# Linear attention into a two-layer tanh-shrink block: moving the phi and the loads of some token groups, and cutting w_out into 128-row loads

## The chip, the cores and the metric

The kernel runs on one core of a Trainium2 chip. The metric is the device time of one execution in microseconds (us). The text calls the engines by short names: PE is TensorE (matrix products), DVE is VectorE, ACT is ScalarE, POOL is GpSimd, SP is SyncE, which here only issues DMAs. POOL also issues DMAs: all loads of inputs. Each engine works off its own instructions in the order in which they were written; semaphores hold an instruction until what it reads is there.

## The reference

Eight batches, eight heads, 576 tokens, 64 features per head. A linear attention is followed by two matrix products over all 4608 tokens:

```python
def phi(x):
    return np.where(x > 0, x, np.exp(x) - 1.0) + 1.0
q_p, k_p = (phi(q), phi(k))
kv = np.einsum('bhsd,bhse->bhde', k_p, v)
z = np.sum(k_p, axis=2)
num = np.einsum('bhsd,bhde->bhse', q_p, kv)
den = np.einsum('bhsd,bhd->bhs', q_p, z)[..., None] + 1e-06
attn = num / den

x = attn.transpose(0, 2, 1, 3).reshape(4608, 512)
h = x @ w_in                  # w_in 512 x 2048
g = h - np.tanh(h)
out = g @ w_out               # w_out 2048 x 512
```

All inputs and the output are float32; the kernel computes in bfloat16 with float32 sums.

## The kernel before

**Chunks.** The 4608 tokens are worked in nine chunks of 512. Chunk c below 8 holds the first 512 tokens of batch c (each partition's first eight of nine tokens); chunk 8 holds the ninth token of every partition for all eight batches, 64 tokens a batch, which the code calls the rest. For batches 0 and 1 the main work leaves the ninth tokens of q out (`main(b)` is J - 1), and they are handled by `load_qr`, `r_phi`, `r_den`, `r_num` and `r_scale` later in the kernel.

**The loop over chunks** (lines 636 to 798). Layer 1 is 16 steps (`fi`, 0 to 15), one for each 128 features of the hidden layer: four matmuls of 128x128 by 128x512 (`l1mm`, line 463), then tanh on ACT and the subtraction on DVE, which give `gT`. From chunk 1 on two steps share one tanh and one subtraction (`l1act2`, lines 469 and 470); in chunk 0 each step has its own (`l1act`, lines 474 and 475). Layer 2 is 16 steps too, each of four matmuls (`l2mm`, line 484): they sum over the 16 blocks of 128 rows of `w_out` into one PSUM bank for each 128 tokens, and ACT copies the finished bank out (`evac`), from where SP stores it. So a layer is 64 large matmuls on PE.

**Work on other batches between the steps.** The lists `s1[i]` and `s2[i]` hold functions that are called behind step i of layer 1 or layer 2. In this way the attention of later batches is spread over the chunks: in chunk c the batch c + 2 gets its phi and its kv products, batch c + 1 its numerators. The position in the lists is the order in which the work stands in each engine's queue. phi is three instructions: exp on ACT (line 156), max and add on DVE (157), min on DVE (158). `a_num` (line 413) makes the numerators of a batch and, in the same place, the kv products of the next; its results lie in PSUM banks 0 to 3 and, for the rest tokens, 6 and 7, and ACT and DVE copy them to `xT`, the input of layer 1. For batches 3 and up the denominators are made by POOL and DVE: `q_prod` (two POOL multiplications, line 242), `q_den` (four DVE sums), `q_scale` (DVE reciprocal and two POOL multiplications, line 256, then the transposing DMA of line 175 that gives `qT`). For batches 0 and 1 PE spreads them (`b0_spread`, `a_spread_pe`), and for batch 2 they go through DRAM (`a_spread`, lines 405 and 408, tile `rdb`).

**Chunk 0** is different: its layer 2 takes its steps from `plan0(s)`, a list of (token block, first w_out block, end). In steps 0 to 3 it takes w_out blocks 0 to 3 for one token block each, in steps 4 to 7 blocks 4 to 7, in 8 and 9 blocks 8 and 9, in 10 and 11 one block for all four token blocks, and in 12 to 15 two blocks for two token blocks. Batch 1's whole attention is put in between these steps: phi of q behind steps 0 and 1, `prepare` (constants for the spreading) behind 2, phi of k behind 4 and 5, transposes of q on PE into banks 4 to 7 behind 5, kv products behind 9, denominators and numerators behind 10, spreading and scaling behind 13. Layer 1 of chunk 0 uses banks 0 to 7 in turn; its steps 12 to 15 use banks 4 to 7.

**Loads.** `load_rest` (line 528) issues on POOL, behind a gate that waits for a DVE instruction of batch 0: the last three quarters of w_in, w_out blocks 0 to 3, q of batch 1, w_out blocks 4 to 7, k of batch 1, blocks 8 and 9, v of batch 1 in two halves, and the last six blocks in four pieces. An issue on POOL waits until the eighth transfer before it has landed. Batches 2 and up are loaded by three issues (k, q, v) from lists: batch 2 behind step 5 of chunk 0's layer 2, batch 3 in chunk 1's layer 1, batch c + 3 behind step 9 of chunk c's layer 2, which for batch 4 is in chunk 1. The tiles `kraw` and `qraw` have one buffer each.

**The rest of batches 0 and 1.** `load_qr` (four issues) stands behind step 10 of chunk 4's layer 2; `r_phi` (one exp, two DVE instructions at lines 329 and 330, a transposing DMA at 332) behind step 9 of chunk 6's layer 1; `r_den` and `r_num` behind `a_num` at step 9 of chunk 6's layer 2. `r_den` writes columns 384 to 447 of bank 7, DVE reads them (line 343), and the result goes through DRAM (lines 348 and 352) to the tile `rdbr`. `r_num` writes columns 128 to 383 of banks 6 and 7. `r_scale`, behind step 3 of chunk 7's layer 1, puts both into `xT`.

Of the kernel before, what the change touches and what calls it, by code (L numbers as in the profile page):

```python
# [18 lines left out]
def kernel(  # L19
# [9 lines left out]
    nc = tc.nc  # L29
    B, H, S, D = q.shape  # L30
# [62 lines left out]
    def load(b, t, src, halves):  # L93

        n = main(b) if src is q else J
        x = src[b].rearrange("h (p j) d -> (h p) (j d)", j=J)[:, 0:n * D]
        if halves:
            y = x.rearrange("(h i q) x -> i q h x", h=2, i=2)
            for i in range(2):
                for hs in ((0, 1), (1, 2)) if i and src is k and b == 0 else ((0, 2),):  # L100
                    nc.gpsimd.dma_start(out=t[:, hs[0]:hs[1], i, 0:n].rearrange("q h j d -> q h (j d)"),
                                        in_=y[i, :, hs[0]:hs[1]])
        else:
            nc.gpsimd.dma_start(out=t[:, :, :, 0:n].rearrange("q h i j d -> q (h i) (j d)"),  # L104
                                in_=x.rearrange("(n q) x -> q n x", n=4))

    def load_k(b):
        k_t[b] = kpool.tile([128, 2, 2, J, D], BF16, name="kraw")
        load(b, k_t[b], k, b == 0)

    def load_q(b):
        q_t[b] = kpool.tile([128, 2, 2, J, D], BF16, name="qraw")
        load(b, q_t[b], q, b == 0)

    def load_v(b):
        load(b, v_b[b % 2], v, b < 2)

    def load_wi(f0, n):

        nc.gpsimd.dma_start(out=w_in_sb[:, :, f0:f0 + n],  # L120
                            in_=moe_w_in[:, f0:f0 + n].rearrange("(t p) f -> p t f", p=128))

    def load_wo(g):
        nc.gpsimd.dma_start(out=w_out_sb[:, 4 * g:4 * g + 4, :],
                            in_=moe_w_out[512 * g:512 * g + 512, :].rearrange("(ko ki) f -> ki ko f", ki=128))


    def load_wof(f0, n):
        nc.gpsimd.dma_start(out=w_out_sb[:, f0:f0 + n, :],
                            in_=moe_w_out[128 * f0:128 * (f0 + n), :].rearrange("(ko ki) f -> ki ko f", ki=128))  # L130
# [33 lines left out]
    def a_kphi(b, i):  # L164
        phi(b, k_t, kp_t, "kp", i)

    def a_qphi(b, i):
        phi(b, q_t, qp_t, "qp", i)
# [37 lines left out]
    def a_vp(b, i, eng=nc.vector):  # L206
        eng.tensor_copy(vp[:, i, :, :, 0:64].rearrange("p j h d -> p h j d"), v_b[b % 2][:, :, i])  # L207
# [320 lines left out]
    def load_rest(r):  # L528
        nc.gpsimd.tensor_copy(rpool.tile([1, 1], BF16, name="g0"), r[0:1, 1, J - 1, 63:64])
        for f0 in (512, 1024, 1536):  # L530
            load_wi(f0, 512)
        load_wo(0)
        load_q(1)
        load_wo(1)
        load_k(1)
        load_wof(8, 2)
        nc.gpsimd.memset(vp[:, :, :, :, 64:66], 1.0)
        load_v(1)
        for f0, n in ((10, 1), (11, 1), (12, 2), (14, 2)):
            load_wof(f0, n)  # L540

# [82 lines left out]

    def plan0(s):

        g, i = divmod(s, 4)
        if g < 2:
            return [(i, 4 * g, 4 * g + 4)]
        if s < 10:  # L630
            return [(n, 8, 10) for n in (2 * i, 2 * i + 1)]
        if s < 12:
            return [(n, s, s + 1) for n in range(4)]
        return [(n, 12 + 2 * (s % 2), 14 + 2 * (s % 2)) for n in (i - i % 2, i - i % 2 + 1)]

    for c in range(NC):
        gT = gpool.tile([128, NF, 512], BF16, name="gT")
# [3 lines left out]
        if c == 0:  # L641
            sub = {}

            def spread1():
                a_spread_pe(1, range(NP))
                for p in range(NP):
                    a_scale(1, p, sub["ns"], p)

            def kv1():
                kv_cols_mm(1, 4, 0)  # L650
                kz_copy(1, 4, 0)

            def num1():
                ns = sub["ns"] = new_ns(1)
                for i in (1, 0):
                    b0 = 4 + 2 * i
                    num_mm(1, i, lambda h: b0 + h)
                    nc.scalar.copy(ns[:, i::2, 0:8, :].rearrange("p a j t -> p a (j t)"), ps_all[:, b0:b0 + 2, :])

            s2[0].append(lambda: a_qphi(1, 0))  # L660
            s2[1].append(lambda: a_qphi(1, 1))
            s2[4].append(lambda: a_kphi(1, 0))
            def k1():
                ek, rk, mk = phi_pieces(1, k_t, kp_t, "kp", 1)
                ek()
                rk()
                a_vp(1, 0)
                mk()
                a_vp1(0, nc.vector.tensor_copy)
                a_vp1(1, nc.scalar.copy)  # L670

            s2[5].append(lambda: ([f() for i in range(2) for f in a_qT_pe(1, i, Banks([4 + 2 * i, 5 + 2 * i]))], k1(),
                                  load_q(2), load_k(2), load_v(2)))
            s2[2].append(prepare)
            s2[9].append(kv1)
            s2[10].append(lambda: (a_den(1, 4), num1(), a_split(1)))
            s2[13].append(spread1)

            qs, ks = [], []

            def exp2(pieces, src, store, name, i):
                pieces.append(phi_pieces(2, src, store, name, i))
                pieces[i][0]()

            def rest2(f):
                f[1]()
                f[2]()

            def k2(i):
                ks.append(phi_pieces(2, k_t, kp_t, "kp", i))  # L690
                ks[i][1]()

            s2[14].append(lambda: exp2(qs, q_t, qp_t, "qp", 0))
            s2[15].append(lambda: (exp2(qs, q_t, qp_t, "qp", 1), rest2(qs[0]), rest2(qs[1]), a_qT_dma(2), [f() for f in later], k2(0), k2(1)))
        elif n1 < B:
            if c == 1:
                def kv2():
                    kv_cols_mm(2, 6, 0)
                    kz_copy(2, 6, 0)

                s1[10].append(kv2)
            if n1 < QS:
                s1[12].append(lambda: (a_den(n1, 6), a_spread(n1)))
            else:
                if c == 2:
                    s1[2].append(lambda: (q_den(n1, 0, 0), q_den(n1, 0, 1)))
                e = 2 * (c == 2)
                s1[3 + e].append(lambda: q_den(n1, 1, 0))
                s1[5 + e].append(lambda: q_den(n1, 1, 1))
                s1[7 + e].append(lambda: q_scale(n1))  # L710
            m = 12 if c == 1 else 9
            s2[m].append(lambda: a_num(n1, n2 if n2 < B else 0))
            if c == B - 4:
                s2[m + 1].append(load_qr)
            if c == B - 2:
                s1[9].append(r_phi)
                s2[m].append(lambda: (r_den(7, 384), r_num(6, 128)))
            if n2 < B:
                s2[m + 2].append(lambda: (q_zb(n2, 4 if c == 1 else 7), q_prod(n2)))
                if c > 1:  # L720
                    s2[15].append(lambda: (q_den(n2, 0, 0), q_den(n2, 0, 1)))
# [8 lines left out]
        if c >= 1 and n2 < B:  # L730
            d = 2
            s2[d].append(lambda: a_kphi(n2, 0))
            s2[d + 2].append(lambda: a_kphi(n2, 1))
            s2[d + 4].append(lambda: a_qphi(n2, 0))
            s2[d + 6].append(lambda: a_qphi(n2, 1))
            for i in range(2):
                s2[d + 1 + 2 * i].append(lambda i=i: a_vp(n2, i))
            if n2 + 1 < B:
                s2[9].append(lambda: (load_k(n2 + 1), load_q(n2 + 1), load_v(n2 + 1)))
        if c == 0:  # L740

            first = Banks([4, 5, 6, 7, 0, 1, 2, 3])
# [34 lines left out]
        os_ = {}  # L777
        for s in range(16):

            (g, i) = divmod(s, 4) if c == 0 else (s % 4, s // 4)  # L780
            if g == 0:
                os_[i] = ps_all[:, i if c == 0 else 4 + i % 2, :]
            if c == NC - 1 and i == 3:

                if g == 0:
                    o2 = ps_all[:, 0, :]
                    for o, f in ((os_[i], slice(0, 384)), (o2, slice(384, DM))):
                        for fi in range(NF):
                            nc.tensor.matmul(o[:, f], gT[:, fi, 384:512], w_out_sb[:, fi, f],
                                             start=(fi == 0), stop=(fi == NF - 1))  # L790
                        evac(c, i, o, f.start, f.stop)
                continue
            for n, f0, f1 in plan0(s) if c == 0 else [(i, 4 * g, 4 * g + 4)]:
                l2mm(gT, os_[n], n, f0, f1)
                if f1 == NF:
                    evac(c, n, os_[n])
            for f in s2[s]:
                f()
# [30 lines left out]
```

## Time and profile before

| | us |
|---|---|
| timed runs, median (lowest to highest of 3) | 286.73 (286.54 to 286.74) |
| the profiled execution, its own time | 289.94 |
| span of that execution, first to last instruction | 288.2 |

The timed runs are other executions than the profiled one. The share of the span in which each engine was busy tells how near each is to its limit; the costliest groups of instructions are the two lines of large matmuls:

```profile
L484 PE MATMUL ps_all<-w_out_sb,gT 128*128 128x512 bf16 x541 | 124.1, 383 | 3.6 <-DVE gT L470 1.9
L463 PE MATMUL ps_all<-xT,w_in_sb 128*128 128x512 bf16 x550 | 122.3, 379 | 0.8 <-DVE xT L434 0.2
```

A row reads: line, engine, operation, output and inputs by the program's names, shape, count, then busy time in us and the mean length of one in ns, then the time for which the engine stood idle just before such instructions and what ended most of it. Matmuls overlap, so the mean of 383 ns is not the distance from one to the next. Some 3% of the matmuls have no record (541 and 550 of 560 each). Where a stretch of the span is shown, times count from the span's start.

Stages of the span by PE's work, in us (layer 1 is L1, layer 2 is L2):

| chunk | L1 from | L1 length | L2 length |
|---|---|---|---|
| 0 | 16.14 | 14.03 | 17.24 |
| 1 | 47.41 | 15.24 | 15.26 |
| 2 | 77.91 | 14.34 | 15.90 |
| 3 | 108.15 | 13.82 | 15.39 |
| 4 | 137.36 | 13.81 | 15.29 |
| 5 | 166.46 | 13.82 | 15.26 |
| 6 | 195.54 | 15.86 | 18.46 |
| 7 | 229.86 | 13.81 | 13.81 |
| 8 | 257.48 | 13.82 | 16.90 to the end |

### The profile page before, as it was taken

How to read it: one execution, taken by the hardware profiler on the slowest of the kernel's cores; microseconds unless marked ns; L12 is line 12 of the kernel's file. 1: busy time of each engine (PE TensorE's matmuls, PEld its weight loads, DVE VectorE, ACT ScalarE, POOL GpSimd, SP SyncE). 2: the span in 40 equal slices, each digit the busy share in tenths (PEclk: the TensorE clock that was granted, in tenths of full speed). 3: DMA queues.
4: the chain of work that ended last, by engine and by line, in shares of the span. 5: the costliest groups of instructions: out<-in, count | busy, mean ns of one | idle time of the engine just before them, and what ended most of it. 6: DMA issues, size and time to landing. Idle time of an engine off the chain costs nothing.

```text
span 288.2 us, 5067 instructions
## 1 busy us (share of the span) xinstructions
PE 275.8 (96%) x2055; PEld 131.6 (46%) x2085; DVE 179.2 (62%) x285; ACT 146.4 (51%) x177; POOL 81.3 (28%) x76
## 2 busy tenths in 40 slices
PE   8899999999999999999999999999977999999996
PEld 2564544444444454445444544454433444444443
DVE  5759877983878737874687468755963066106700
ACT  4747658856256735674556455654622156116511
POOL 8642220510544253514351744014410000000000
PEclk9999999999999999999999999999999799999999
DMA  7999999799990897069605990522053210131023
GB/s 106 182 206 207 206 206 196 162 193 190 257 226 11 99 210 170 0 122 212 143 0 118 174 203 1 121 56 55 0 100 75 73 38 2 36 73 36 2 61 85
DMA packets 40087, 33.25 MB, mean 115 GB/s; under 512 B 17696, under 2 KB 35776, under 8 KB 39936
## 3 DMA queue, kind: packets, MB, share of 16 engines
q0 software_dynamic: 18640, 18.35, 40.1%
q1 hardware_dynamic: 21424, 14.58, 21.8%
q8 instruction: 16, 0.26, 0.4%
q14 instruction: 7, 0.06, 0.1%
HBM read 38.14 MB, written 9.46 MB: 165 GB/s over the span
## 4 chain that ended last, share of the span: by engine, by line
PE 74%; DMA 12%; DVE 6%; issue 2%; ACT 2%; POOL 1%; SPq 1%; DVEq 0%; POOLq 0%
PE ps_all L463 37%; PE ps_all L484 32%; DMA v<-in_v_dram 3%; DMA rdb<-ds 3%; DVE gT L470 2%; DMA out_dram<-osb 2%; DMA qT<-qp 2%; DMA ds<-rden 2%; PE ps_all L203 1%; PE ps_all L750 1%; PE ps_all L284 1%; ACT th L469 1%; DVE xT L434 1%; DVE qpr L330 1%; ACT osb L495 1%
## 5 line engine op out<-in xcount | busy, mean ns | idle before, releaser
L484 PE MATMUL ps_all<-w_out_sb,gT 128*128 128x512 bf16 x541 | 124.1, 383 | 3.6 <-DVE gT L470 1.9
L463 PE MATMUL ps_all<-xT,w_in_sb 128*128 128x512 bf16 x550 | 122.3, 379 | 0.8 <-DVE xT L434 0.2
L470 DVE TENSOR_TENSOR gT<-ps_all,th 128x1024 bf16<-128x1024 f32 x64 | 77.6, 1217 | 46.1 <-ACT th L469 46.1
L469 ACT ACTIVATE th<-ps_all 128x1024 f32<-128x1024 f32 x64 | 65.6, 1025 | 48.7 <-PE ps_all L463 46.1
L463 PEld LDWEIGHTS <-w_in_sb 128*128 128x128 bf16 x560 | 54.6, 98 | 66.2 <-issue 1.0
L484 PEld LDWEIGHTS <-gT 128*128 128x128 bf16 x560 | 54.3, 99 | 66.4 <-issue 4.6
L495 ACT COPY osb<-ps_all 128x512 f32<-128x512 f32 (+1 forms) x36 | 20.8, 583 | 61.5 <-PE ps_all L484 49.4
L256 POOL TENSOR_TENSOR qp<-qp,rd 128x1152 bf16<-128x1152 bf16 x10 | 21.0, 2124 | 39.0 <-issue 23.1
L242 POOL TENSOR_TENSOR pr<-qp,zb 128x1152 f32<-128x1152 bf16 x10 | 23.5, 2372 | 18.8 <-ACT zb L235 18.8
L247 DVE TENSOR_REDUCE dn<-pr 128x9 f32<-128x576 f32 x20 | 14.5, 745 | 12.8 <-POOL pr L242 12.8
L156 ACT ACTIVATE e<-qraw 128x1152 bf16<-128x1152 bf16 (+1 forms) x16 | 18.1, 1135 | 3.2 <-DMA qraw<-in_q_dram 3.2
L156 ACT ACTIVATE e<-kraw 128x1152 bf16<-128x1152 bf16 x15 | 17.4, 1162 | 2.2 <-DMA kraw<-in_k_dram 2.2
L158 DVE TENSOR_TENSOR qp<-e,r 128x1152 bf16<-128x1152 bf16 (+1 forms) x16 | 11.9, 742 | 4.3 <-ACT e L156 3.2
L158 DVE TENSOR_TENSOR kp<-e,r 128x1152 bf16<-128x1152 bf16 x15 | 11.4, 760 | 4.7 <-ACT e L156 3.9
L104 POOL DMA_DIRECT2D kraw<-in_k_dram x7 | 5.4, 772 | 30.3 <-ACT e L156 14.1
L425 DVE CAST xT<-ps_all 128x1024 bf16<-128x1024 f32 x5 | 6.1, 1217 | 7.1 <-PE ps_all L293 7.1
L570 PE MATMUL ps_all<-zero 128*128 128x512 bf16 x28 | 8.5, 457 | 1.3 <-DVE zero L518 1.2
L104 POOL DMA_DIRECT2D qraw<-in_q_dram x7 | 5.5, 780 | 11.9 <-ACT e L156 7.1
L475 DVE TENSOR_TENSOR gT<-ps_all,th 128x512 bf16<-128x512 f32 x12 | 7.9, 688 | 0.9 <-ACT th L474 0.2
L207 DVE COPY vp<-v 128x1152 bf16<-128x1152 bf16 x11 | 5.7, 518 | 4.2 <-DMA v<-in_v_dram 4.2
L474 ACT ACTIVATE th<-ps_all 128x512 f32<-128x512 f32 x12 | 7.2, 598 | 2.3 <-DVE gT L756 1.0
L157 DVE TENSOR_SCALAR r<-qraw 128x1152 bf16<-128x1152 bf16 (+1 forms) x16 | 7.6, 476 | 0.3 <-DMA qraw<-in_q_dram 0.3
(109 smaller groups left out, 146.5 us busy)
## 6 DMA issues: line engine op xcount, KB each, us to landing
out_dram<-osb SPq DMA_DIRECT2D x65, 128.0 KB, 2.4
kraw<-in_k_dram POOLq DMA_DIRECT2D x7, 576.0 KB, 7.8
qraw<-in_q_dram POOLq DMA_DIRECT2D x6, 576.0 KB, 9.6
v<-in_v_dram POOLq DMA_DIRECT2D x6, 576.0 KB, 11.9
w_in_sb<-in_moe_w_in_dram POOLq DMA_DIRECT2D x3, 512.0 KB, 10.6
v<-in_v_dram POOLq DMA_DIRECT2D x4, 288.0 KB, 12.4
rdb<-ds SPq DMA_DIRECT2D x2, 576.0 KB, 5.8
w_out_sb<-in_moe_w_out_dram POOLq DMA_DIRECT2D x2, 512.0 KB, 16.0
```

The source lines that it names most:

```text
L104: nc.gpsimd.dma_start(out=t[:, :, :, 0:n].rearrange("q h i j d -> q (h i) (j d)"), in_=x.rearrange("(n q) x -> q n x", n=4))
L156: return (lambda: nc.scalar.activation(e, x, AF.Exp), lambda: nc.vector.tensor_scalar(r, x, 0.0, 1.0, ALU.max, ALU.add), lambda: nc.vector ...
L158: lambda: nc.vector.tensor_tensor(y, e, r, ALU.min))
L242: nc.gpsimd.tensor_mul(pr_t[b][:, i].rearrange("p j h d -> p j (h d)"), qp_t[b][:, i].rearrange("p j h d -> p j (h d)"), zb_t[b][:, i].uns ...
L247: nc.vector.tensor_reduce(dn_t[b][:, i, :, h], pr_t[b][:, i, :, h, :], mybir.AxisListType.X, ALU.add)
L256: nc.gpsimd.tensor_mul(x, x, rd[:, i].unsqueeze(2).to_broadcast([128, J * 2, D]))
L463: nc.tensor.matmul(h, w_in_sb[:, p, fi * 128:(fi + 1) * 128], xT[:, p, c * 512:(c + 1) * 512], start=(n == 0), stop=(n == NP - 1))
L469: nc.scalar.activation(th, h, AF.Tanh)
L470: nc.vector.tensor_sub(gT[:, fi:fi + 2, :], h, th)
L484: nc.tensor.matmul(o, gT[:, fi, i * 128:(i + 1) * 128], w_out_sb[:, fi, :], start=(fi == 0), stop=(fi == NF - 1))
L495: nc.scalar.copy(osb[:, f0:f1], o[:, f0:f1])
L570: nc.tensor.matmul(ps_all[:, 0, :], zero[:, 0:128], zero, start=True, stop=True)
```

## The change

Three places are changed.

1. The rest tokens of batches 0 and 1: `load_qr` goes from chunk 4's layer 2 to behind step 12 of chunk 3's layer 1; `r_phi` goes from chunk 6's layer 1 to behind step 1 of chunk 4's layer 2; `r_den` and `r_num` stay at step 9 of chunk 6's layer 2 but stand ahead of `a_num`.
2. Batch 4's three loads go from behind step 9 to behind step 15 of chunk 1's layer 2, so behind batch 3's `q_prod` in POOL's queue.
3. Chunk 0's layer 2 takes one 128-row block of w_out for all four token blocks in each of the steps 0 to 11; steps 12 to 15 stay. The loads follow: ten w_out transfers in place of seven, with q of batch 1 ahead of w_out. Batch 1's phi of q goes behind steps 13 and 14 of chunk 0's layer 1, its phi of k behind steps 0 and 3 of layer 2, its transposes behind step 2, `prepare` behind 4, the copies of v behind 6 and 8, and batch 2's three loads behind 2, 3 and 8.

```diff
@@ def load
-            for i in range(2):
+            for i in halves:
...
-        load(b, k_t[b], k, b == 0)
+        load(b, k_t[b], k, (0, 1) if b == 0 else ())
...
-    def load_v(b):
-        load(b, v_b[b % 2], v, b < 2)
+    def load_v(b, parts=(0, 1)):
+        load(b, v_b[b % 2], v, parts if b < 2 else ())
...
@@ def load_rest
-        load_wo(0)
         load_q(1)
-        load_wo(1)
+        load_wof(0, 3)
         load_k(1)
-        load_wof(8, 2)
         nc.gpsimd.memset(vp[:, :, :, :, 64:66], 1.0)
-        load_v(1)
+        for f0, n in ((3, 1), (4, 2), (6, 2)):
+            load_wof(f0, n)
+        load_v(1, (0,))
+        for f0 in (8, 9):
+            load_wof(f0, 1)
+        load_v(1, (1,))
         for f0, n in ((10, 1), (11, 1), (12, 2), (14, 2)):
             load_wof(f0, n)
...
     def plan0(s):
-        g, i = divmod(s, 4)
-        if g < 2:
-            return [(i, 4 * g, 4 * g + 4)]
-        if s < 10:
-            return [(n, 8, 10) for n in (2 * i, 2 * i + 1)]
         if s < 12:
             return [(n, s, s + 1) for n in range(4)]
-        return [(n, 12 + 2 * (s % 2), 14 + 2 * (s % 2)) for n in (i - i % 2, i - i % 2 + 1)]
+        i = 2 * (s // 14)
+        return [(n, 12 + 2 * (s % 2), 14 + 2 * (s % 2)) for n in (i, i + 1)]
...
@@ chunk 0
-            s2[0].append(lambda: a_qphi(1, 0))
-            s2[1].append(lambda: a_qphi(1, 1))
-            s2[4].append(lambda: a_kphi(1, 0))
...
-            s2[5].append(lambda: ([f() for i in range(2) for f in a_qT_pe(1, i, Banks([4 + 2 * i, 5 + 2 * i]))], k1(),
-                                  load_q(2), load_k(2), load_v(2)))
-            s2[2].append(prepare)
+            s1[13].append(lambda: a_qphi(1, 0))
+            s1[14].append(lambda: a_qphi(1, 1))
+            s2[0].append(lambda: a_kphi(1, 0))
+            s2[2].append(lambda: ([f() for i in range(2) for f in a_qT_pe(1, i, Banks([4 + 2 * i, 5 + 2 * i]))], load_q(2)))
+            s2[3].append(lambda: (a_kphi(1, 1), load_k(2)))
+            s2[4].append(prepare)
+            s2[6].append(lambda: a_vp(1, 0))
+            s2[8].append(lambda: (vp1(), load_v(2)))
...
@@ chunks 1 to 7
+            if c == 3:
+                s1[12].append(load_qr)
+            if c == 4:
+                s2[1].append(r_phi)
+            if c == B - 2:
+                s2[m].append(lambda: (r_den(7, 384), r_num(6, 128)))
             s2[m].append(lambda: a_num(n1, n2 if n2 < B else 0))
-            if c == B - 4:
-                s2[m + 1].append(load_qr)
-            if c == B - 2:
-                s1[9].append(r_phi)
-                s2[m].append(lambda: (r_den(7, 384), r_num(6, 128)))
...
-                s2[9].append(lambda: (load_k(n2 + 1), load_q(n2 + 1), load_v(n2 + 1)))
+                s2[15 if c == 1 else 9].append(lambda: (load_k(n2 + 1), load_q(n2 + 1), load_v(n2 + 1)))
```

More of the change, by code (lines that the diff above doesn't have):

```diff
@@ L108, in load_k @@
         k_t[b] = kpool.tile([128, 2, 2, J, D], BF16, name="kraw")
-        load(b, k_t[b], k, b == 0)
+        load(b, k_t[b], k, (0, 1) if b == 0 else ())
     def load_q(b):
         q_t[b] = kpool.tile([128, 2, 2, J, D], BF16, name="qraw")
-        load(b, q_t[b], q, b == 0)
-    def load_v(b):
-        load(b, v_b[b % 2], v, b < 2)
+        load(b, q_t[b], q, (0, 1) if b == 0 else ())
+    def load_v(b, parts=(0, 1)):
+        load(b, v_b[b % 2], v, parts if b < 2 else ())
     def load_wi(f0, n):
@@ L121, in load_wi @@
                             in_=moe_w_in[:, f0:f0 + n].rearrange("(t p) f -> p t f", p=128))
-    def load_wo(g):
-        nc.gpsimd.dma_start(out=w_out_sb[:, 4 * g:4 * g + 4, :],
-                            in_=moe_w_out[512 * g:512 * g + 512, :].rearrange("(ko ki) f -> ki ko f", ki=128))
     def load_wof(f0, n):
@@ L658, in num1, with vp1 @@
                     nc.scalar.copy(ns[:, i::2, 0:8, :].rearrange("p a j t -> p a (j t)"), ps_all[:, b0:b0 + 2, :])
-            s2[0].append(lambda: a_qphi(1, 0))
-            s2[1].append(lambda: a_qphi(1, 1))
-            s2[4].append(lambda: a_kphi(1, 0))
[L663 to L668, printed above, removed]
+            def vp1():
                 a_vp1(0, nc.vector.tensor_copy)
                 a_vp1(1, nc.scalar.copy)
-            s2[5].append(lambda: ([f() for i in range(2) for f in a_qT_pe(1, i, Banks([4 + 2 * i, 5 + 2 * i]))], k1(),
-                                  load_q(2), load_k(2), load_v(2)))
-            s2[2].append(prepare)
+            s1[13].append(lambda: a_qphi(1, 0))
[6 more added lines that the diff above has]
+            s2[8].append(lambda: (vp1(), load_v(2)))
             s2[9].append(kv1)
@@ L778 @@
         for s in range(16):
-            (g, i) = divmod(s, 4) if c == 0 else (s % 4, s // 4)
-            if g == 0:
-                os_[i] = ps_all[:, i if c == 0 else 4 + i % 2, :]
+            g, i = s % 4, s // 4
+            if c == 0 and s == 0:
+                os_ = {n: ps_all[:, n, :] for n in range(4)}
+            elif c > 0 and g == 0:
+                os_[i] = ps_all[:, 4 + i % 2, :]
             if c == NC - 1 and i == 3:
```

## The prediction

> **What bounds the kernel now.** I read the engine table first, then matrix-engine work stage by stage, then the waits of that engine, and only then what the other engines do around the two long waits.
>
> ```profile
> span 288.2 us, 5067 instructions
> PE 275.8 (96%) x2055; PEld 131.6 (46%) x2085; DVE 179.2 (62%) x285; ACT 146.4 (51%) x177; POOL 81.3 (28%) x76
> PEclk9999999999999999999999999999999799999999
> ```
>
> TensorE (PE) is busy for 96% of the span, so only what stops or slows PE can count. One of the 40 slices has a lower granted clock. I cut the span where PE goes from one layer to the next and compare like with like: chunk 5's layer 1, chunk 6's layer 1, chunk 5's layer 2, chunk 6's layer 2 (columns: stretch, length, busy time of each engine, granted clock, DMA share, GB/s).
>
> ```profile
> 166.46:180.28 13.82, 13.77 (x65) 6.28 (x65) 10.71 (x13) 7.76 (x8) 6.49 (x4) 1.00 0.54 94
> 180.28:195.54 15.26, 15.05 (x153) 7.29 (x154) 9.34 (x17) 8.57 (x11) 2.96 (x3) 1.00 0.44 92
> 195.54:211.40 15.86, 13.93 (x64) 6.24 (x64) 13.62 (x15) 8.28 (x9) 6.51 (x3) 1.00 0.09 19
> 211.40:229.86 18.46, 16.76 (x103) 7.56 (x105) 4.49 (x6) 3.97 (x6) 0.00 (x0) 0.91 0.43 95
> ```
>
> A layer is 64 large matmuls; 13.82 us is 0.216 us each, and layer 1 of chunks 3, 4, 5, 7 and 8 takes 13.81 or 13.82. Chunk 6 takes 2.04 us more in layer 1, and its layer 2 takes 3.20 more than chunk 5's although it has less side work (no kv products). No other layer from chunk 2 on loses 0.6 us. The timeline of chunk 6 shows why (start, length, engine, line, what, count, wait before it):
>
> ```profile
> 205.69 4.24 POOL L256 TENSOR_TENSOR qp<-qp,rd 128x1152 bf16<-128x1152 bf16 x2 [7.89 <-issue]
> 206.57 1.39 DVE L329 TENSOR_SCALAR r<-qr 128x512 bf16<-128x512 bf16 x1
> 208.06 2.15 DVE L330 TENSOR_TENSOR qpr<-e,r 128x512 bf16<-128x512 bf16 x1
> 211.40 8.79 PE L484 MATMUL ps_all<-w_out_sb,gT 128*128 128x512 bf16 x39 [1.88 <-DVE gT L470]
> ...
> 222.06 0.29 PE L340 MATMUL ps_all<-qTr,kz 128*32 128x64 bf16 x8 [1.25 <-ACT xT L426]
> 222.73 0.32 PE L293 MATMUL ps_all<-qTr,kz 64*64 64x64 bf16 x15 [0.24 <-DVE denr L343]
> 223.21 6.81 PE L484 MATMUL ps_all<-w_out_sb,gT 128*128 128x512 bf16 x23 [0.16 <-issue]
> ```
>
> Three things: the two VectorE (DVE) steps of r_phi take 3.54 us while GpSimd (POOL) does q_scale, and layer 2 waits 1.88 for gT; r_den waits 1.25 for a_num's last copy; then 24 large matmuls (one record is missing) take 6.81 us and not 24 x 0.216 = 5.18. The clock tells the last one:
>
> ```profile
> 222.00:223.40 1.40, 0.95 (x25) 0.69 (x26) 0.98 (x4) 0.01 (x1) 0.00 (x0) 0.99 0.00 0
> 223.40:226.78 3.38, 3.38 (x9) 1.22 (x8) 0.00 (x0) 0.52 (x1) 0.00 (x0) 0.50 0.08 25
> 226.78:229.86 3.08, 3.08 (x16) 1.37 (x15) 0.00 (x0) 0.07 (x1) 0.00 (x0) 1.00 0.55 144
> ```
>
> For 3.38 us the granted clock is 0.50: 1.69 us lost.
>
> **The change, part by part.**
>
> *r_phi from chunk 6 to chunk 4.* In chunk 6 nothing is left on DVE but what chunk 5's layer 1 has too, so I take that twin row: 15.86 - 13.82 = **-2.04 us**. In chunk 4 it stands after step 1 of layer 2. There POOL's q_scale is over at 151.71 (starts 147.51, 4.20 long) and DVE's last subtraction ends at 153.65, so the two don't meet. Cost there: ACT 0.62 (its row in chunk 6), DVE by the 1152-wide rows scaled to 512 elements: 0.45 x 512/1152 + 0.76 x 512/1152, about 0.54 us. ACT next waits 1.38 us for an output row, DVE 0.89 and 0.74 us for exponentials, so it is hidden: 0. With that cover gone, say at the contended 3.54 us, kp of batch 6 (done 157.26) would still come before its products at 160.41 or some 0.4 late: 0 to +0.4. On SP, the small transpose (1.24 us of issue) stands behind chunk 4's large one (151.73 to 154.47) and ahead of the first output store, which goes some 0.3 us later into one of five buffers: 0.
>
> The Trainium skill, "SBUF — State Buffer", section "SBUF: two separate sides", says that GpSimd and a VectorE instruction with two SBUF inputs or in a two-port mode lock each other out for a whole instruction. The rows agree: r ends within 0.2 us of POOL's first multiply, qpr within 0.3 of the second. [...]
>
> *load_qr from chunk 4 to chunk 3.* Its four issues take 2.87 us of POOL (161.70 on). Behind q_scale of chunk 3 POOL is idle 5.05 us (122.51 to 127.56), so they fit; landing took some 10 us and the first reader is 30 us off. The transpose of chunk 3 beside them lands after 4.7 us where 8 are left. 0.
>
> *r_den and r_num ahead of a_num.* The banks that r_den takes are then free, so the 1.25 us wait for a_num's copies goes; the 0.24 us wait on denr stays (DVE is idle there, as before: 7.07 us). **-1.25 us**. Next late could be rdbr: its DRAM round trip takes some 6.5 us from denr, and r_scale comes six steps of layer 2 and four of layer 1 later, about 9 us.
>
> *The half clock.* It follows the stretch 219.9 to 223.2 in which PE waited and ran only 64-wide products. With the 1.25 us gone that stretch looks like the kv stretch of the other chunks, behind which the clock stays 1.00. **-1.69 us**, bounds -1.69 and 0.
>
> The Trainium skill, "TensorE: Matmul & The Clock Gate", Part 1, has half rate as the state after an idle window of about 3.4 us, and lets the window run free of the kernel. The trace agrees on 0.50 and 3.38 us. By the free window timed runs may lack this half clock, and the sum without it is 1.69 us smaller.
>
> *Batch 4's loads behind batch 3's products.* Three issues (2.23 us of POOL) move from 71.97 and 75.10 to behind q_prod, which ends at 82.40. They land by median rows at 82.4 + 7.8, 83.2 + 9.6 and 83.9 + 11.9: 90.2, 92.8 and 95.8; the readers come at 93.37, 97.45 and 95.88. What could gain is rdb of batch 2, for which DVE waits until 76.98 and PE loses 0.53 us (chunk 2's layer 1 is 14.34). But rdb keeps the DMA engines full by itself from 70 us on. I take 0; bounds -0.5 (the wait gone) and +0.3 (v late by half a microsecond, partly covered by DVE's gaps).
>
> *Chunk 0.* PE now works as follows (column 2 is the length), with no wait over 0.2 us, so there is nothing to gain for PE:
>
> ```profile
> 16.14:30.17 14.03, 13.98 (x79) 7.75 (x80) 11.10 (x20) 9.36 (x15) 3.97 (x8) 1.00 1.24 207
> 30.17:47.41 17.24, 16.87 (x190) 8.31 (x192) 13.39 (x34) 10.65 (x14) 3.60 (x5) 1.00 1.22 206
> ```
>
> The loads run as one full stream (DMA share above 1.2), and each lands behind the one before by its size: 512 KB 2.55 us, 576 KB 2.85, 288 KB 1.43, 256 KB 1.27, 128 KB 0.63. I add these in the new order from 24.7 (third w_in piece, issued 12.1, landed after 12.6): q of batch 1 27.2, w_out blocks 0 to 2 29.1, k 32.0, block 3 32.6, 4-5 33.9, 6-7 35.1, v's first half 36.6, block 8 37.2, 9 37.8, v's second half 39.2, then 39.9, 40.5, 41.8, 43.0 as before. Each issue waits 0.3 us past the landing of the eighth before it (w_out 10 starts at 24.95, that piece lands at 24.7); in the new order the eight in flight still hold over 7 us of stream, so it doesn't run dry. PE wants them, at 0.864 us a step from 30.17, with 0.89 for the transposes after step 2 and the rest as now: block 3 at 33.65, 4 at 34.5, 6 at 36.2, 8 at 38.0, 9 at 38.8, 10 at 40.5. Least margin 0.6 us: no wait. The row order of matmuls costs nothing, as steps 10 and 11 have it already.
>
> What moves is phi. On ACT two exponentials (1.05 each) go ahead of the last two tanh, which end at about 32.6 and not 30.97. DVE then ends the last subtraction at 33.6 (sub 13 to 30.07, r and min 31.2, sub 31.9, r and min 33.0, sub 33.6). The transposes now come at 32.77, and their last four want that subtraction's bank at 33.43: 0.2 us of wait. An r of phi slows by 0.24 beside a POOL issue (0.66 for 0.42 at 32.74). **+0.3 us**, bounds 0 and +0.9. kv follows at 40.2; its last copies of v end at 39.7 to 40.1, so it hardly waits, and from step 9 on all stands as before.
>
> **Sum.** -2.04 - 1.25 - 1.69 + 0.3 = -4.68: span 288.2 to 283.5, and the profiled execution 289.94 to 285.3. The timed median, 286.73, is 3.21 us below that execution; its rows are not seen. Taken off it: **282.0 us**.
>
> **Rivals.** (1) *No half clock in the timed runs.* For it: it is one event of one execution, which is 3.21 us longer than the timed ones, and 1.69 of that could be this. Against: the waits that go before it are part of every execution. The sum is then -2.99: 283.7 us. (2) *Slower: small loads cost more than their bytes.* Place: chunk 0's steps 3 to 13, where eleven transfers from block 3 on must each land within a fraction of a microsecond. Were each 0.6 us later than its size says, the last comes 6.6 us late with 1.4 of margin (wanted at 44.4): PE waits 5.2, and 282.0 + 5.2 = 287.2 us. It decides from (4.7 + 1.4) / 11 = 0.55 us each. Against: 128 KB pieces land 0.63 apart, the same 200 KB/us as 512 KB ones. (3) *DVE's new place is tight.* If phi and prepare in chunk 0 slip behind kv by 1 us more than I see, and v of batch 4 by 0.3, the time is 283.3; it still is faster.
>
> The Trainium skill, "DMA: Bandwidth & Descriptors", "Anatomy of one DMA", gives some 2 us fixed for each transfer and advises pieces of 1 MiB. That speaks against ten w_out transfers in place of seven: by it, an estimate, three more would cost 6 us if nothing overlapped, and the time would be 288. The rows above show the overlap.
>
> **How the numbers follow.** Main case 0.70 (280.6 to 283.0: the lower end if in timed runs the first wait brings a half clock too, which it doesn't in the profile), rival 1 has 0.18, rival 3 0.06, rival 2 0.06. The range reaches from 280.6 to 284.4: it holds the main case, rivals 1 and 3 with chunk 0's upper bound. Within 0.2%, some 0.57 us and about what a measurement of this kernel can tell from no change, only a third of rival 2 falls. Faster 0.94, same 0.02, slower 0.04.
>
> **What would show it.** Layer 1 of chunk 6 at 13.8; its layer 2 at 15.5 with clock 1.00; r_phi's DVE steps of 0.2 to 0.4 us in chunk 4; the wait before chunk 2's layer 1 as now; a short wait at the transposes of chunk 0. I am wrong if PE waits for w_out or vp between 33 and 45 us, if the half clock only moves elsewhere, or if r_phi meets POOL again.

## The result and the profile after

The changed kernel takes 283.12 us (median of 6 runs, 283.02 to 283.76); the kernel before, timed beside it, 287.02 us over its 6 runs (286.54 to 290.23). The ratio is 0.985 with a 95% interval of 0.981 to 0.990, so the change is worth 1.0% to 1.9%. In three more groups of runs the kernel before had medians of 287.30, 287.47 and 288.16 us, and in each of them single runs of 291 or 292 us. With each timed run goes its mean granted clock: 1.00 in most, 0.994 in some. One half clock of 3.41 us makes that difference (1.7 us lost of 288).

The page of the changed kernel, engine table and clock row:

```profile
span 281.5 us, 5103 instructions
PE 276.1 (98%) x2085; PEld 131.0 (47%) x2085; DVE 176.9 (63%) x285; ACT 146.0 (52%) x177; POOL 81.9 (29%) x79
PEclk9999999999999999999999999999999999999999
```

PE's busy time is nearly what it was (276.1 for 275.8 us, with 30 more matmul records); the span is 6.7 us shorter. So in the main waits went and not work, and the slice with the lower clock is gone. By stages (stretch, length, busy time of PE, weight loads, DVE, ACT and POOL, granted clock, DMA share, GB/s): chunk 0's layer 2, chunk 2's two layers, chunk 4's layer 2 with r_phi in it, chunk 6's two layers.

```profile
29.75:47.12 17.37, 17.31 (x193) 8.34 (x192) 13.26 (x34) 9.80 (x14) 4.74 (x7) 1.00 1.22 205
...
77.63:91.45 13.82, 13.82 (x66) 6.27 (x65) 11.60 (x17) 7.75 (x8) 8.52 (x6) 1.00 0.74 126
91.45:106.74 15.29, 15.29 (x155) 7.31 (x154) 9.54 (x17) 8.56 (x11) 7.11 (x7) 1.00 0.98 163
149.77:165.06 15.29, 15.29 (x156) 7.32 (x154) 10.29 (x19) 9.08 (x12) 5.23 (x6) 1.00 0.92 164
194.14:207.95 13.81, 13.81 (x65) 6.24 (x64) 10.67 (x13) 7.76 (x8) 5.91 (x3) 1.00 0.08 19
207.95:223.22 15.27, 15.10 (x106) 7.00 (x105) 4.17 (x6) 3.96 (x6) 0.53 (x1) 1.00 0.43 96
```

Chunk 6 gives 2.05 and 3.19 us, chunk 2 gives 0.52 and 0.61, the stretch ahead of chunk 0's layer 1 gives 0.36, and chunk 0's two layers take 0.07 more: 6.66 of the 6.7. Not all of this is the change: the execution of before that was profiled was a long one (see e8 below). Chunk 4's layer 2 carries 0.98 us more of DVE and 0.52 more of ACT at the same length.

The two timelines that answer to those shown of before: r_phi in chunk 4, and r_den, r_num and a_num in chunk 6 (start, length, engine, line, what, count, wait before it).

```profile
146.10 4.19 POOL L251 TENSOR_TENSOR qp<-qp,rd 128x1152 bf16<-128x1152 bf16 x2 [7.88 <-issue]
...
152.16 0.28 DVE L324 TENSOR_SCALAR r<-qr 128x512 bf16<-128x512 bf16 x1
152.55 0.43 DVE L325 TENSOR_TENSOR qpr<-e,r 128x512 bf16<-128x512 bf16 x1
```

```profile
216.68 0.29 PE L335 MATMUL ps_all<-qTr,kz 128*32 128x64 bf16 x8
216.90 0.21 PE L288 MATMUL ps_all<-qTr,kz 64*64 64x64 bf16 x1
217.28 0.32 PE L288 MATMUL ps_all<-qTr,kz 64*64 64x64 bf16 x15 [0.17 <-DVE denr L338]
217.41 0.62 PE L279 MATMUL ps_all<-qT,kz 64*64 64x512 bf16 x8
```

The same two DVE instructions that took 1.39 and 2.15 us take 0.28 and 0.43 where POOL's multiplications have ended 1.9 us before. r_den (L335) starts with no wait.

### The profile page after: what moved, and what is told of

It is laid out like the page before. It is cut to its first block, busy times and chain, and to the rows that moved or that the text cites. A ratio compares the mean times of both kernels' runs of the same rounds, so it can differ in the third digit from the quotient of the medians.

```text
span 281.5 us, 5103 instructions
## 1 busy us (share of the span) xinstructions
PE 276.1 (98%) x2085; PEld 131.0 (47%) x2085; DVE 176.9 (63%) x285; ACT 146.0 (52%) x177; POOL 81.9 (29%) x79
## 4 chain that ended last, share of the span: by engine, by line
PE 91%; DMA 4%; DVE 1%; ACT 1%; issue 1%; POOL 1%; SPq 0%; DVEq 0%; POOLq 0%
PE ps_all L458 43%; PE ps_all L479 41%; DMA out_dram<-osb 3%; DMA kraw<-in_k_dram 2%; PE ps_all L198 2%; PE ps_all L742 1%; PE ps_all L279 1%; ACT osb L490 1%; SPq L503 0%; PE ps_all L309 0%; POOL qraw L101 0%; ACT e L151 0%; PE ps_all L182 0%; PE ps_all L371 0%; DVE rden L380 0%
## 5 line engine op out<-in xcount | busy, mean ns | idle before, releaser
L568 PE MATMUL ps_all<-zero 128*128 128x512 bf16 x29 | 9.2, 475 | 1.2 <-DVE zero L513 1.2
L124 POOL DMA_DIRECT2D w_out_sb<-in_moe_w_out_dram x10 | 6.4, 637 | 10.1 <-DMA w_in_sb<-in_moe_w_in_dram 4.7
L420 ACT CAST xT<-ps_all 128x1024 bf16<-128x1024 f32 x5 | 5.1, 1012 | 5.1 <-PE ps_all L288 4.4
```

The lines of the kernel that those rows point to most:

```text
L568: nc.tensor.matmul(ps_all[:, 0, :], zero[:, 0:128], zero, start=True, stop=True)
```

## The experiments

Twelve more kernels were run, three of them repeats: e8 and e9 of the kernels before and after, e10 of e4. The stages below are from each one's profile, in us; "front" is the time up to layer 1 of chunk 0, "half clock" names where 3.41 us at a granted clock of 0.50 stand.

| kernel | front | chunk 0 L2 | chunk 1 L1 | chunk 2 L1, L2 | chunk 6 L1, L2 | half clock |
|---|---|---|---|---|---|---|
| before | 16.14 | 17.24 | 15.24 | 14.34, 15.90 | 15.86, 18.46 | chunk 6 |
| before again (e8) | 15.91 | 17.24 | 15.31 | 13.81, 15.29 | 15.86, 16.77 | none |
| changed | 15.78 | 17.38 | 15.24 | 13.81, 15.29 | 13.81, 15.27 | none |
| changed again (e9) | 17.02 | 17.43 | 15.24 | 13.81, 15.29 | 13.81, 15.27 | none |
| e1, rest tokens alone | 16.38 | 17.24 | 16.19 | 14.52, 15.29 | 13.81, 15.26 | none |
| e2, batch 4's loads alone | 16.29 | 17.24 | 15.25 | 13.81, 15.29 | 15.86, 16.77 | none |
| e3, chunk 0 alone | 16.40 | 17.44 | 16.19 | 13.81, 15.29 | 15.86, 16.77 | none |
| e4, all but batch 4's loads | 16.22 | 17.38 | 15.27 | 13.82, 15.29 | 13.81, 15.26 | none |
| e10, as e4 | 15.85 | 17.38 | 15.24 | 14.52, 15.29 | 13.81, 15.27 | none |
| e5, r_phi meets POOL | 15.64 | 17.62 | 15.24 | 14.03, 15.29 | 13.81, 15.26 | none |
| e6, r_phi in chunk 6 | 16.09 | 17.39 | 15.24 | 13.99, 15.29 | 13.81, 15.27 | none |
| e7, r_den behind a_num | 15.53 | 17.42 | 15.52 | 14.04, 15.29 | 13.81, 16.77 | none |
| e11, all but chunk 0 | 18.04 | 17.24 | 16.94 | 13.81, 15.29 | 13.81, 15.26 | front |
| e12, gate in chunk 1 | 16.60 | 17.37 | 15.24 | 13.84, 16.36 | 13.81, 15.26 | none |

Chunk 0's layer 2 and chunk 6 follow the kernel. The other columns differ between executions of one and the same kernel.

**Each part alone.** e1 is the kernel before with the rest-token part:

```diff
+            if c == 3:
+                s1[12].append(load_qr)
+            if c == 4:
+                s2[1].append(r_phi)
+            if c == B - 2:
+                s2[m].append(lambda: (r_den(7, 384), r_num(6, 128)))
             s2[m].append(lambda: a_num(n1, n2 if n2 < B else 0))
-            if c == B - 4:
-                s2[m + 1].append(load_qr)
-            if c == B - 2:
-                s1[9].append(r_phi)
-                s2[m].append(lambda: (r_den(7, 384), r_num(6, 128)))
```

> The kernel before with the rest-token part alone (load_qr in chunk 3, r_phi in chunk 4, r_den and r_num ahead of a_num). My theory: chunk 6 carries the gain, so layer 1 of chunk 6 at 13.8 (15.86 before), its layer 2 at 15.3 to 15.5 (18.46 before) with clock 1.00, and the time is 3.3 us below the kernel before where that has no half clock and some 5 us below where it has one. Rival, that the loads share in it: chunk 6 keeps 1 us or more, or the time is less than 2.5 us below.

284.07 us for 287.30, ratio 0.988 (0.986 to 0.990), with chunk 6 at 13.81 and 15.26. As far as these runs can tell, this part alone carries the change.

e2 moves batch 4's loads alone, and e4 and e10 undo that move in the changed kernel:

```diff
-                s2[9].append(lambda: (load_k(n2 + 1), load_q(n2 + 1), load_v(n2 + 1)))
+                s2[15 if c == 1 else 9].append(lambda: (load_k(n2 + 1), load_q(n2 + 1), load_v(n2 + 1)))
```

> The kernel before with batch 4's loads behind step 15 of chunk 1's layer 2 alone. Theory A, the later loads free the DMA engines for rdb and for the stores: layer 1 of chunk 2 at 13.8 (14.34 before) and its layer 2 at 15.3 (15.90 before), time 1.1 us below. Theory B, the 1.1 us in chunk 2 differ from one execution to the next whatever the loads do: chunk 2 may show the waits again or not, time within 0.5 us of the kernel before. Chunk 6 keeps its 15.9 and some 16.7 to 18.5.

288.12 us for 287.30, ratio 1.003 (1.000 to 1.007). Chunk 2 is at its best here, which theory A asked for; but so it is in e8 and e3, where the loads stand as before. The median is 0.8 us above the kernel before, more than the 0.5 that theory B allowed: five of the ten runs have a mean clock of 0.994 or lower, and the other five have a median of 287.09. Theory B, with that reserve.

> The changed kernel with batch 4's loads back behind step 9 of chunk 1's layer 2. Theory A (the later loads relieve rdb and qT): chunk 2 at 14.3 and 15.9 again, time 1.1 us above the changed kernel. Theory B (chance): chunk 2 at 13.8 to 14.3 and 15.3 to 15.9 without a pattern, time within 0.4 us of the changed kernel.

284.12 us, ratio 0.989 (0.987 to 0.991), chunk 2 at 13.82 and 15.29: theory A falls, since the waits ought to be back.

> As e4, now timed on the same chip as the changed kernel. Theory B (batch 4's loads are worth nothing): within 0.4 us of e9. Theory A (they relieve rdb): 0.5 to 1.1 us above e9.

284.01 us, with e9 at 284.83 beside it on the same chip; the ratios are 0.984 (0.979 to 0.989) and 0.988 (0.983 to 0.992). This time chunk 2's layer 1 took 14.52. Where DVE waits for rdb, 7.7 to 8.2 us pass from rdb's second issue to DVE's start on it, with the loads in the old place (before: 69.04 to 76.98) as in the new one (e5: 68.30 to 76.48), so by these rows the loads don't slow rdb. The wait comes and goes with either place. Its three longest cases, 0.5 to 0.7 us of PE, all have the old place (before, e1, e10), where the new place shows 0.23 at most; a small worth of the move isn't excluded, but no median shows one.

e3 has chunk 0's part alone (loads, plan0, places of batch 1's phi), e11 all but it.

> The kernel before with chunk 0's part alone (w_out by blocks, phi of batch 1 earlier). My theory: layer 2 of chunk 0 at 17.3 to 17.5 (17.24 before), no other stage moves, time within 0.4 us of the kernel before. Rival, that the early phi relieves chunks 1 and 2: chunk 2's layers at 13.8 and 15.3, time about 1 us below.

287.28 us for 287.30, ratio 1.001 (0.998 to 1.004). Chunk 0's layer 2 took 17.44; chunk 1's layer 1 took 16.19, which neither theory had.

> The changed kernel with chunk 0 as before (loads, layer 2 and phi of batch 1). If chunk 0's part costs its 0.14 to 0.38 us at the transposes and gives nothing back, this is 0.1 to 0.4 us below e9. If the early phi or the finer loads steady chunks 1 and 2, it is above e9 and its runs are wider apart.

284.67 us (283.78 to 287.10) for e9's 284.83 (284.41 to 286.61): no difference beyond the spread. The profiled execution is the longest of them, 287.10, and its rows show two reasons: half clock in the front, and 16.94 in chunk 1.

**Why r_phi's steps were long.** e5 takes the changed kernel and puts r_phi where POOL is at work, in a chunk where it had not been in layer 1 before:

```diff
             if c == 4:
-                s2[1].append(r_phi)
+                s1[9].append(r_phi)
```

> The changed kernel with r_phi in chunk 4 as now, but behind step 9 of layer 1, where POOL does q_scale. My theory (r_phi's two DVE steps wait for POOL's multiplications, wherever they stand): they take 1.4 and 2.1 us, layer 1 of chunk 4 takes 15.9 (13.82 in the changed kernel), time 2 us above the changed kernel. Rival (it was chunk 6's load, not POOL): they take 0.2 and 0.4 us and chunk 4 stays at 13.8.

The timeline of e5 in chunk 4, DVE's rows and then POOL's:

```profile
147.27 1.39 DVE L324 TENSOR_SCALAR r<-qr 128x512 bf16<-128x512 bf16 x1
148.76 2.15 DVE L325 TENSOR_TENSOR qpr<-e,r 128x512 bf16<-128x512 bf16 x1
...
146.39 4.24 POOL L251 TENSOR_TENSOR qp<-qp,rd 128x1152 bf16<-128x1152 bf16 x2 [7.88 <-issue]
```

The lengths are those of chunk 6 before, to the hundredth of a microsecond; layer 1 of chunk 4 takes 15.86 us (13.81 in the changed kernel), and the time is 285.58 us (285.35 to 285.62), ratio 0.994 (0.993 to 0.996). e6 does the reverse, r_phi in chunk 6 but ahead of POOL's multiplications:

```diff
-            if c == 4:
-                s2[1].append(r_phi)
+            if c == 6:
+                s1[5].append(r_phi)
```

> The changed kernel with r_phi back in chunk 6's layer 1, but behind step 5, where POOL is idle. My theory: its DVE steps take 0.2 to 0.4 us, layer 1 of chunk 6 takes 13.8 to 14.1, time within 0.4 us of the changed kernel. Rival (chunk 6's DVE queue has no room for r_phi): layer 1 of chunk 6 takes 14.5 or more.

DVE's timeline rows of e6 in chunk 6:

```profile
202.92 0.28 DVE L324 TENSOR_SCALAR r<-qr 128x512 bf16<-128x512 bf16 x1
203.31 0.42 DVE L325 TENSOR_TENSOR qpr<-e,r 128x512 bf16<-128x512 bf16 x1
```

Chunk 6 stays at 13.81, 283.64 us, ratio 0.988 (0.986 to 0.989). So it isn't the chunk and isn't room in DVE's queue: it is POOL.

**The order of r_den, and the half clock.**

```diff
-            if c == B - 2:
-                s2[m].append(lambda: (r_den(7, 384), r_num(6, 128)))
             s2[m].append(lambda: a_num(n1, n2 if n2 < B else 0))
+            if c == B - 2:
+                s2[m].append(lambda: (r_den(7, 384), r_num(6, 128)))
```

> The changed kernel with r_den and r_num behind a_num again. My theory: the wait of 1.25 us before r_den is back, layer 2 of chunk 6 takes 16.5 without a half clock and 18.2 with one; time 1.25 or 2.9 us above the changed kernel, and not the same in every run if the half clock depends on more than the wait. Rival (the half clock needs r_phi's wait too): 16.5 and clock 1.00 in every run.

PE's rows of e7 in chunk 6:

```profile
217.41 0.23 PE L288 MATMUL ps_all<-qT,kz 64*64 64x64 bf16 x8
218.89 0.29 PE L335 MATMUL ps_all<-qTr,kz 128*32 128x64 bf16 x8 [1.25 <-ACT xT L421]
219.11 0.21 PE L288 MATMUL ps_all<-qTr,kz 64*64 64x64 bf16 x1
219.56 0.31 PE L288 MATMUL ps_all<-qTr,kz 64*64 64x64 bf16 x15 [0.24 <-DVE denr L338]
```

The 1.25 us are back to the digit, and layer 2 of chunk 6 takes 16.77 us with the clock at 1.00. The median is 285.17 us, ratio 0.994 (0.992 to 0.997). Eight of its ten runs lie between 284.85 and 285.49, two at 287.41 (mean clock 0.994) and 287.56 (1.00).

> The kernel before, unchanged, profiled once more. If chunk 2's waits (0.53 and 0.61 us) belong to the kernel, they stand there again; if they are chance, one or both are gone. The half clock behind chunk 6's waits should stand there in some runs (mean clock 0.994) and not in others, and the times differ by 1.7 us between the two.

This execution of the unchanged kernel took 286.90 us. Both waits of chunk 2 are gone, the half clock too. Its rows of DVE and POOL in chunk 6:

```profile
204.14 1.18 DVE L470 TENSOR_TENSOR gT<-ps_all,th 128x1024 bf16<-128x1024 f32 x1
205.23 1.39 DVE L329 TENSOR_SCALAR r<-qr 128x512 bf16<-128x512 bf16 x1
206.72 2.15 DVE L330 TENSOR_TENSOR qpr<-e,r 128x512 bf16<-128x512 bf16 x1
...
204.35 4.24 POOL L256 TENSOR_TENSOR qp<-qp,rd 128x1152 bf16<-128x1152 bf16 x2 [7.89 <-issue]
```

r_phi's two long steps stand to the digit, and chunk 6 takes 15.86 and 16.77. DVE's subtraction from PSUM (gT), which starts just ahead of POOL's multiplications and runs into them, keeps its 1.2 us. Among the five profiles with the 1.25 us wait (before, e2, e3, e7, e8) one has a half clock behind it.

The mean clocks of the timed runs tell how often it comes. Of the 90 runs on record of kernels with r_den behind a_num (three groups of before, e2, e3, e7, e8) 20 have a mean clock of 0.994 or lower; of the 46 of kernels with r_den ahead (the changed kernel, e1, e4 to e6, e9 to e12) 2 have, and one of these is e11's in the front. Where in a run the half clock stood is on record for the profiled executions alone. So the change removes most half clocks, though most runs had none. Whether it is r_den's wait or r_phi's that brings them isn't shown: e7, with r_den's alone, has 1 in 10 runs, and e5, with r_phi's alone (in chunk 4), none in 4. The 20 runs lie 1.3 to 5.9 us above the median of the others of their group, the two longest with a mean clock of 0.988; half clocks of 1.7 us are a part of that, and where the rest goes isn't shown.

> The changed kernel, unchanged, once more beside the next three. 283.0 to 283.8 us in most runs; chunk 6 at 13.8 and 15.3; chunks 1 and 2 from 15.24 and 13.81 upward by chance.

284.83 us (284.41 to 286.61) for 288.16, ratio 0.988 (0.983 to 0.992): chunk 6 and chunk 0 as expected. The time is above the expected 283.0 to 283.8; in this group the kernel before is higher too, and in e9's profile the front takes 17.02 for 15.78.

**A wait that turned up: chunk 1.** In e1 and e3 layer 1 of chunk 1 took 0.95 us more. Rows of DVE and POOL in e3:

```profile
51.12 1.77 DVE L152 TENSOR_SCALAR r<-kraw 128x1152 bf16<-128x1152 bf16 x2
...
51.23 2.66 POOL L202 COPY vp<-v 128x1152 bf16<-128x1152 bf16 x2 [12.47 <-DVE qp L153]
```

Two such r take 0.82 us elsewhere; here POOL's copies of batch 2's v start between them, and the second r takes 1.40. The row names DVE's qp as what ended POOL's wait, but v landed at 51.09, and in all thirteen profiles without e12's gate POOL starts 0.14 or 0.15 us behind v's landing. DVE's next subtraction is late by that, and PE waits 0.9 for it.

Which of the two starts first decides. In e1 and e3 POOL's copies start at 51.09 and 51.23, ahead of the second r (51.27 and 51.49). In the ten profiles with short r they start behind it, in e9 by 0.01 us: there r keeps its 0.45, and POOL's first copy takes 1.45 in place of 1.14. That a profile has the long r is chance: up to this place e1 and e11 run the same code as before, and e3 that of the changed kernel.

In e11 the copies met two other steps of DVE (timeline, all engines):

```profile
51.25 2.47 POOL L207 COPY vp<-v 128x1152 bf16<-128x1152 bf16 x2 [9.29 <-PE ps_all L463]
51.32 1.40 DVE L157 TENSOR_SCALAR r<-qraw 128x1152 bf16<-128x1152 bf16 x1
...
52.83 1.51 DVE L158 TENSOR_TENSOR qp<-e,r 128x1152 bf16<-128x1152 bf16 x1
...
56.26 1.02 PE L463 MATMUL ps_all<-xT,w_in_sb 128*128 128x512 bf16 x4 [1.68 <-DVE gT L470]
```

e12 lets POOL begin only when the second r of k has ended:

```diff
-            s1[0].append(lambda: (a_vp(2, 0, nc.gpsimd), a_vp(2, 1, nc.gpsimd),
+            s1[0].append(lambda: (nc.gpsimd.tensor_copy(rpool.tile([1, 1], BF16, name="g0"), r_t[2][0:1, 1, J - 1, 63:64]),
+                                  a_vp(2, 0, nc.gpsimd), a_vp(2, 1, nc.gpsimd),
```

> The changed kernel with one tiny POOL copy ahead of POOL's two copies of v of batch 2 in chunk 1, which reads the last element of DVE's second r of k of batch 2, so POOL can't begin before that r has ended. My theory (the wait in chunk 1 of e1 and e3, 0.95 us, comes where v lands before the second r and POOL's copy holds it up): both r at 0.45 us, layer 1 of chunk 1 at 15.24, median 0 to 0.3 us below e9 with the highest runs gone. Rival (chunk 1's wait has another source): no difference from e9.

The timeline of e12, POOL's rows and then DVE's:

```profile
52.14 0.18 POOL L720 COPY g<-r 1x1 bf16<-1x1 bf16 x1 [13.04 <-DVE r L152]
52.26 2.22 POOL L202 COPY vp<-v 128x1152 bf16<-128x1152 bf16 x2
...
51.25 0.82 DVE L152 TENSOR_SCALAR r<-kraw 128x1152 bf16<-128x1152 bf16 x2
```

POOL waited for DVE's r and not for v, both r took 0.82, chunk 1's layer 1 15.24. The median is 283.82 us for e9's 284.83, ratio to the kernel before 0.984 (0.979 to 0.988) for e9's 0.988 (0.983 to 0.992). The intervals overlap, its highest run, 285.18, is the profiled one, which waited 1.0 us for qT in chunk 2, and e10, without the gate, took 284.01 in the same group. So the mechanism is shown; that e12 is the faster kernel isn't.

## Why the prediction was right, and where it was off

- **r_phi, -2.04 us**: measured -2.05, in every kernel that has r_phi away from POOL's multiplications. The reason holds both ways (e5 and e6). The Trainium skill, "SBUF — State Buffer", "SBUF: two separate sides", says that GpSimd and a VectorE step with two SBUF inputs or in a two-port mode lock each other out, and that the one that starts first keeps the other waiting. e5 agrees for qpr, which has two SBUF inputs (2.15 us beside POOL, 0.42 in e6), and chunk 1 for who starts first; that r, with one input, grows because it is in such a mode isn't shown, only that it grows (1.39 for 0.28). In chunk 4 the steps take 0.28 and 0.43 us where the width-scaled estimate had 0.20 and 0.34; the cover hid them.
- **r_den ahead of a_num, -1.25 us**: measured -1.50 (16.77 to 15.27 in e7 and the changed kernel). The wait was sized right. The wait on denr shrank by 0.07. The rest, 0.18, is by the rows mostly overlap: behind the start of r_num's last 15 matmuls PE starts the next ones 0.13 us later (217.28 to 217.41), where in e7 it took 0.25 (219.56 to 219.81).
- **Half clock, -1.69 us: this is the step that failed.** The prediction took an event of one execution as part of every execution: "the waits that go before it are part of every execution". The waits are; the half clock followed them in one profile of five, and by the mean clocks a half clock stands in 20 of 90 runs with that wait and in 2 of 46 without. A median holds none of it. So the 3.21 us between the profiled and the timed runs, taken off at the end, already held these 1.69 us, and the sum took them off twice. In the median the term is 0; in the mean it is some 0.3 us, an estimate (20/90 less 2/46, times 1.7). The Trainium skill, "TensorE: Matmul & The Clock Gate", Part 1, lets the window in which the clock is set run free of the kernel; that fits a half clock that comes in some runs of one kernel and not in others, in e11 even in the front (granted 0.50 from 13.8 us on, front 18.04 us), while the two rates show that the kernel has a part in it. Which part stays open: ahead of the half clock PE was busy for 1.78 of 3.42 us (219.96 to 223.38 in before), but it was so for 1.74 of 3.42 from 209.72 on too, and there the clock stayed at 1.00.
- **3.21 us between profiled and timed runs**: the profiled execution of before was a long one. Beside e8 (286.90 us) it had 1.69 us of half clock, 0.53 + 0.61 in chunk 2 and 0.23 in the front, together 3.06, where 3.04 us lie between the two. (The prediction said that no other layer from chunk 2 on loses 0.6 us; chunk 2's layer 2 lost 0.61, 15.90 for 15.29.) Between e8 and the profiled execution of the changed kernel lie 3.61 us, and the stages add up to it: 2.05 and 1.50 in chunk 6, 0.13 in the front and 0.07 in chunk 1, less 0.14 in chunk 0. The measured 283.12 lies just above the main case's 280.6 to 283.0. With the half clock left out of the sum, rival 1's 283.7 us stands 0.6 above it; the forecast, 282.0, stands 1.1 below. r_den's 0.25 and chunk 0's 0.16 make 0.4 of those 0.6; the rest stays open.
- **Batch 4's loads, 0**: no run contradicts it (e2, e4 and e10). v of batch 4 landed at 93.3 us, ahead of its reader at 95.1, not at the feared 95.8. "The wait before chunk 2's layer 1 as now" did not come: 13.81 us for 14.34; by e8 it can be absent without the change.
- **Chunk 0, +0.3 us**: measured +0.13 to +0.38 (17.37 to 17.62 for 17.24). In the changed kernel the 0.14 stands at the transposes, 1.03 us to the next large matmul where before had 0.89, as foreseen. The stream of loads ran as added up, and PE has no wait for w_out in any profile. Rival 2 asked for 0.55 us more per transfer; the last w_out piece landed at 42.7, as before (43.0).
- **Rival 3** did not come. What was missed altogether is that POOL and DVE also meet in chunk 1, by chance, in three of fourteen profiles.

## What to carry to other kernels

When an off-path instruction that should take 0.3 us takes five times that, look at what the other engine does in the same microseconds, and move it to where that engine is idle: here 0.7 us of DVE work cost PE 2 us. A step that several things can hold up (a wait, a clock, a landing) should be read from two executions before it enters a sum: what stands in one of them alone is a chance and gets a probability, and the mean clock of each timed run, where it is on record, tells how large. Cutting loads finer in a full stream cost no wait here, and was also worth nothing, because nothing had waited for them.

## What was not expected of the hardware

DVE steps on bf16 that meet POOL's 1.15 to 2.1 us instructions grow from 0.28, 0.43 and 0.45 us to 1.39, 2.15 and 1.40, while DVE's subtractions from PSUM beside the same POOL work keep 1.2 us. The front, up to layer 1, took from 15.5 to 18.0 us over fourteen profiles with the same matmuls in it; the 18.0 holds a half clock, and the longest front without one is 17.0.
